# Fox attention and bilinear FFN: the late batches' scores in three TensorE visits instead of four

## The chip, the cores and the metric

The kernel runs on one core of one Trainium2 chip. The metric is the device time of one execution in microseconds (us); lower is better. The time before is the median of three runs, 402.83 us (400.74 to 403.5).

## The reference

Forgetting attention over 8 batches of 8 heads, 576 positions and 64 dimensions, followed by a bilinear feed-forward network (FFN) over the 4608 tokens:

```
scores = scale * np.matmul(q, k.transpose(0, 1, 3, 2))
cum = np.cumsum(np.log(np.clip(f, 0.0001, 1.0)), axis=-1)
scores = np.where(causal, -1000000000.0, scores + cum[:, :, :, None] - cum[:, :, None, :])
attn = exp(scores - max) / (sum + 1e-09)
x = (attn @ v)  as [4608, 512]
out = ((x @ w_a) * (x @ w_b)) @ w_out          # 512 -> 1536 -> 512
```

## The kernel before

**Tiles.** A *unit* `u` is four heads of one batch (`b, hh = divmod(u, 2)`), so there are two units for each batch; a *pair* `t` is two heads, two pairs to a unit. The 576 query positions of a head are cut into four blocks of 128 rows (blocks 0 to 3) and a tail of 64 rows (block 4). Block i needs the keys 0 to 128(i+1), the tail needs all 576. Each head's 64 dimensions lie as two halves of 32 partitions, and the four heads of a unit sit in the four 32-row groups of the array, so that the score products of the four heads run abreast.

**Visits.** TensorE computes a unit's scores in visits (`qk_group(u, g)`, matmuls at L399). `groups = [(1, 0), (2,), (3,), (4,)]` says which blocks a visit holds, so a unit takes four visits, in the order 0, 1, 3, 2 from batch 2 on. A visit writes two PSUM tiles of two banks each (`sc`, a ring of two, so one visit holds all four `sc` banks until its scores are read). The other four banks are the ring `ff`: FFN products, transposes, value products. From batch 3 on the value product of the pair's tail (`pv4`, L634) is written into 64 spare columns of the first visit's tile.

**Softmax.** Batches 0 to 2 (`DIRECT`) add the decay and the mask with further matmuls (`pick`, `low`), and VectorE takes a row maximum (L486). From batch 3 on VectorE reads the scores out of PSUM, adds the decay from the SBUF tile `spread` and takes the maximum in one custom operation (`do_decay`, L510; two for each block and pair, one for each head), into a tile `S` in SBUF; that operation is what releases the PSUM banks. ScalarE takes the exponentials (L542, L548), VectorE the reciprocals of the sums, GpSimd normalises (L565) and masks the decay rows (L460 to L471). The probabilities are transposed by DMA, and TensorE multiplies them with the values (`pv`, L609, L611), VectorE or ScalarE evicts.

**FFN.** For each block of tokens (256, 384 or 512) and each of 12 slices of 128 hidden columns TensorE makes `psa` and `psb` (four matmuls each, L872), ScalarE or VectorE copies `psa` to fp16 (L138, L142), VectorE multiplies with `psb` (L888), and 36 output rows of 12 matmuls follow (`pso`, L897). A `psa` or `psb` needs a free `ff` bank; a bank comes free with the copy or the multiplication.

**Order.** All of the work is cut into numbered operations. `ORDER` is a table of these numbers that sets, by hand, the order in which they are issued on all engines; `CHOICE` gives the engine of each operation that could go to several. Forty `fill` operations (four matmuls on an identity each, L178) are placed in it too; they compute nothing that is used. Each engine works through its own list in order.

Of the kernel before, what the change touches and what calls it, by code (L numbers as in the profile page):

```python
# [37 lines left out]
def kernel(  # L38
# [61 lines left out]
    RING = {"S": 2, "bc": 4, "n32": 3, "n16": 2, "PA": 3, "PB": 2, "PTA": 2, "PTB": 2, "st": 8, "ht": 15, "a16": 3, "osb": 2, "ff": 4}  # L100
# [88 lines left out]
    def f_tiles():  # L189
        x = [s_pool.tile([128, 1024], FP32, tag="S", name=n) for n in ("cum_f", "cum_l")]  # L190
        cw["f"], cw["l"] = x[0][HP[0], 0:S], x[1][HP[0], 0:S]
        cw["1"] = x[0][:, S:].bitcast(FP16)[:, 0:S]
# [112 lines left out]
    def batch_inputs(b):  # L305
# [4 lines left out]
        for which, part, gm in items:  # L310
            gate = qk_ops[(2 * (b - 1) + gm // 4, gm % 4)][-1:] if b >= EARLY else []
# [61 lines left out]
    groups = [(1, 0), (2,), (3,), (4,)]  # L373

# [12 lines left out]
    def qk_group(u, g):  # L387
        b, hh = divmod(u, 2)
        qT, kT = T[("T", "q", b)], T[("T", "k", b)]
        rows = crow[b // 2] if b < DIRECT else None  # L390
        if single(u, g):
            c = [[ps.tile([128, 512], FP32, tag="ff", bufs=RING["ff"], name=f"sc{g}") for _ in range(2)] for _ in range(2)]
        else:
            c = [ps.tile([128, 2, 512], FP32, tag="sc", bufs=2, name=f"sc{g}") for _ in range(2)]
        heads = [(c[w] if g == 3 else [c[w][0], c[w][1]] if single(u, g) else [c[w][:, 0, :], c[w][:, 1, :]],
# [5 lines left out]
        if g == 3:  # L401
            for x, lo, hi in ((0, 0, SF), (1, SF, S)):
# [3 lines left out]
            for x, lo, hi in ((0, 0, SF), (1, SF, S)):  # L406
                if b < DIRECT:
                    for y, h, r, n in heads:
                        mm(y[HP[h], x, 0:hi - lo], pick[r, n:n + 1].to_broadcast([32, 64]), rows[r, lo:hi], stop=True)
            if b < DIRECT:  # L410
                for a in range(2):
                    for y, h, r, _ in heads:
                        mm(y[HP[h], 1, 32 * a:32 * a + 32], low[r, a, 0:64], neg[r, :], stop=True)
            for w in range(2):
                T[("s", NP * b + 2 * hh + w, 4)] = c[w].rearrange("p a k -> p (a k)")[:, 0:S]
            return
        t0 = 2 * u
        col, n_ = 0, 0
        for i in groups[g]:
# [16 lines left out]
            if b < DIRECT and i == groups[g][-1]:  # L436
                m = len(groups[g])
                lo = 0 if turned(t0, groups[g][0]) else col - 128 * m
                hi = 128 if m == 1 and lo == 0 else col
                for a in range(4):  # L440
                    for y, h, r, _ in heads:
                        x = y[h][:, lo:hi].rearrange("p (m k) -> p m k", k=128)
                        x = x[:, 0:3:2] if hi - lo == 384 else x
# [3 lines left out]
        if g == 0 and not single(u, g):  # L447
            for w in range(2):
                T[("spare", t0 + w)] = c[w][:, 0, 448:512]
# [39 lines left out]
    def do_decay(t, g, i, h):  # L489
        st, c = stats(t), spread[t % RING["bc"]]  # L490
        if ("S", t, g) not in T:
            T[("S", t, g)] = s_pool.tile([128, 1024], FP32, tag="S", name="S")
            col = 0
            for x in groups[g]:
# [6 lines left out]
        else:  # L501
            n = 128 * (i + 1)
            o, x, y = T[("z", t, i)][:, h * n:h * n + n], T[("s", t, i)][:, h, :], c[:, h, SM:SM + n]
# [15 lines left out]
    def p_tile(t, part):  # L519
# [4 lines left out]
        if ("P", "A", t) not in T and t in IN_S:  # L524
            x = s_pool.tile([128, 1024], FP32, tag="S", name="S").bitcast(FP16)
# [137 lines left out]
    def softmax(t, g, qk, sc, rows, st_users, pu, norms):  # L663
# [4 lines left out]
        for i in groups[g]:  # L668
            part = part_of(t, i)
            mxs = []  # L670
            for h in range(1 if direct else 2):
                if direct:
                    mx = op("D", f"max{i}" + ("s" if sc[0] is not sc[1] else ""), lambda _, i=i: do_max(t, i), [qk])
# [17 lines left out]
                for x in sc if direct else sc[h:h + 1]:  # L691
# [3 lines left out]
            for h in range(1 if i == 4 else 2):  # L695
                ex = op("A", f"exp{i}", lambda _, i=i, h=h: do_exp(t, i, h), mxs if i == 4 or direct else mxs[h:h + 1])
                if direct:
                    ex.deps.append(o_e)
                    sc[h].append(ex)
# [26 lines left out]
    def attention(u):  # L726
# [5 lines left out]
        turn = (0, 1, 3, 2)  # L732
        for g in turn:
# [3 lines left out]
            qk = op("E", f"qk{g}" + ("d" if b < DIRECT else ""), lambda _, g=g: qk_group(u, g), deps)  # L737
# [6 lines left out]
            sc_of[g] = [take(qk, "sc") for _ in range(2)]  # L744
            for w in "qk":
                T_users[(w, b)].append(qk)
            if g == 0 and (u - 1) // 2 >= EARLY:
                old = [t - 2 for t in ts]
                for x, t in enumerate(old):
                    pv4 = op("E", "pv4", lambda _, t=t: do_pv4(t, T.pop(("spare", t + 2))), [qk, *late[t][0]])  # L750
                    sc_of[0][x].append(pv4)
                    behind.append((pv4, x))
                    pv = op("E", "pv", lambda _, t=t: do_pv(t, (0, 1, 2, 3)), [qk, *late[t][0]])
                    late[t][1](pv, pv4, sc_of[0][x])
        for w, t in enumerate(ts):
            for g in turn:
                softmax(t, g, qk_ops[(u, g)][0], [sc_of[g][w]] * 2, bc[t], st_users, pu, norms)
        for pv4, x in behind:
            pv4.deps.extend(o for o in sc_of[0][x] if o.kind[:3] in ("dec", "max", "exp"))
# [374 lines left out]
```

## Time and profile before

| | before |
|---|---|
| median of three runs | 402.83 us (400.74 to 403.5) |
| the profiled execution | 402.96 us, span 401.2 us |
| busy TensorE / VectorE / ScalarE / GpSimd | 386.0 / 315.3 / 250.0 / 255.1 us |
| attention ends on TensorE at | about 345 us, then FFN alone |

The span is the time from the first to the last instruction; the profiled execution's own time is 1.8 us longer. Start times in the timeline count from the span's start, and a matmul's listed duration includes its pipeline, so that what a group costs is read from start to start.

### The profile page before, as it was taken

The page shows a single profiled execution, that of the slowest core. Times are in us where ns is not written, and L with a number is a line of the kernel's source. Part 1 is how long each engine was busy: PE and PEld are TensorE (multiplying, and loading weights), DVE is VectorE, ACT ScalarE, POOL GpSimd, SP SyncE. Part 2 cuts the span into 40 slices and gives each one's busy share as a digit, 9 for nine tenths or more (in the row PEclk, how much of TensorE's full clock was granted, in tenths as well). Part 3 has the DMA queues.
Part 4 walks back from the last instruction along what each step waited for, and adds up shares of the span by engine and source line. Part 5 has one row for each costly group of instructions (what it writes and reads, how often), then busy time and mean ns, then how long its engine had stood idle before and what let it go on. Part 6 is the DMA issues. An engine that isn't in the chain of part 4 may idle for free.

```text
span 401.2 us, 11066 instructions
## 1 busy us (share of the span) xinstructions
PE 386.0 (96%) x4040; PEld 213.8 (53%) x4040; DVE 315.3 (79%) x908; ACT 250.0 (62%) x755; POOL 255.1 (64%) x425
## 2 busy tenths in 40 slices
PE   6788999989999999999999999999999999999996
PEld 6666776856755544444445444544454444444554
DVE  8789998978959889997989879789978792462560
ACT  4887876566657667868785778677868783201011
POOL 4888777988478777889597859697777472000000
PEclk9659999999999999999999999999999999999999
DMA  7999789999999898999999999989998629100102
GB/s 279 194 246 265 129 218 283 219 192 231 223 218 209 225 191 242 228 292 219 288 216 299 225 255 276 252 206 256 206 218 181 132 53 205 38 2 36 70 1 79
DMA packets 148311, 78.22 MB, mean 195 GB/s; under 512 B 130592, under 2 KB 133408, under 8 KB 148256
## 3 DMA queue, kind: packets, MB, share of 16 engines
q1 hardware_dynamic: 144416, 72.66, 77.2%
q0 software_dynamic: 3696, 4.72, 7.3%
q8 instruction: 31, 0.51, 0.5%
q14 instruction: 24, 0.20, 0.1%
q10 hardware_dynamic: 144, 0.13, 0.1%
HBM read 49.69 MB, written 9.58 MB: 148 GB/s over the span
## 4 chain that ended last, share of the span: by engine, by line
PE 80%; DVE 7%; DMA 7%; POOL 2%; issue 1%; SPq 1%; ACT 1%; DVEq 0%; POOLq 0%; ACTq 0%
PE pso L897 22%; PE psb L872 21%; PE psa L872 20%; PE sc L399 8%; DVE st L486 2%; PE pv L609 2%; DMA v<-in_v_dram 2%; PE idle L178 2%; DMA PTB<-PB 2%; DMA xT<-spread 1%; PE pv L621 1%; PE pv L611 1%; PE psP L589 1%; DMA k<-in_k_dram 1%; PE sc L634 1%
## 5 line engine op out<-in xcount | busy, mean ns | idle before, releaser
L872 PE MATMUL psb<-xT,wb 128*128 128x512 f16 (+2 forms) x528 | 115.2, 341 | 1.5 <-ACT osb L138 1.1
L872 PE MATMUL psa<-xT,wa 128*128 128x512 f16 (+2 forms) x528 | 115.2, 341 | 0.2
L897 PE MATMUL pso<-wout,ht 128*128 128x512 f16 (+1 forms) x444 | 98.0, 374 | 0.0
L565 POOL TENSOR_SCALAR PA<-PA,st 128x128 f16<-128x128 f16 (+2 forms) x162 | 75.8, 484 | 30.7 <-DVE st L557 20.5
L510 DVE CUSTOM_DVE_ANT_0 S<-sc,spread 128x128 f32<-128x128 f32 (+3 forms) x160 | 86.5, 568 | 7.5 <-PE sc L399 3.3
L888 DVE TENSOR_TENSOR ht<-psb,a 128x512 f16<-128x512 f32 (+2 forms) x132 | 76.6, 587 | 14.8 <-PE psb L872 9.9
L138 ACT CAST a<-psa 128x512 f16<-128x512 f32 (+2 forms) x85 | 44.1, 525 | 51.8 <-PE psa L872 50.0
L872 PEld LDWEIGHTS <-wb 128*128 128x128 f16 x528 | 49.8, 98 | 43.5 <-issue 4.3
L872 PEld LDWEIGHTS <-wa 128*128 128x128 f16 x528 | 49.7, 98 | 42.8 <-issue 3.0
L548 ACT ACTIVATE PA<-S,st 128x256 f16<-128x256 f32 (+2 forms) x120 | 60.1, 503 | 14.4 <-DVE st L510 13.0
L897 PEld LDWEIGHTS <-ht 128*128 128x128 f16 x444 | 41.8, 98 | 46.7 <-issue 0.6
L565 POOL TENSOR_SCALAR PB<-PB,st 128x512 f16<-128x512 f16 (+1 forms) x84 | 58.8, 716 | 11.7 <-DVE st L557 8.1
L486 DVE TENSOR_REDUCE st<-sc 128x2 f32<-128x512 f32 (+8 forms) x68 | 47.1, 726 | 8.5 <-PE sc L399 5.9
L399 PE MATMUL sc<-kT,qT 32*128 32x128 f16 (+5 forms) x960 | 42.4, 274 | 4.9 <-DVE qT L302 2.7
L399 PEld LDWEIGHTS <-qT 32*128 32x128 f16 (+1 forms) x960 | 18.6, 96 | 28.3 <-issue 13.9
L548 ACT ACTIVATE PB<-S,st 128x512 f16<-128x512 f32 x40 | 28.5, 714 | 6.3 <-DVE st L510 6.1
L557 DVE RECIPROCAL st<-st 128x2 f32<-128x2 f32 x128 | 18.2, 157 | 14.0 <-ACT PB L548 6.8
L142 DVE CAST a<-psa 128x256 f16<-128x256 f32 (+2 forms) x47 | 25.1, 534 | 4.6 <-PE psa L872 3.9
L142 POOL CAST k<-k 128x1152 f16<-128x1152 f32 (+1 forms) x15 | 20.9, 1393 | 10.8 <-DMA k<-in_k_dram 7.4
L565 POOL TENSOR_SCALAR spread<-spread,st 128x128 f16<-128x128 f16 (+4 forms) x36 | 19.8, 561 | 6.6 <-DVE st L557 5.0
L138 ACT CAST xT<-pv 128x512 f16<-128x512 f32 (+2 forms) x36 | 16.0, 465 | 12.6 <-PE pv L611 6.3
L460 POOL TENSOR_SCALAR_AFFINE_SELECT spread<-spread 128x768 f32<-128x768 f32 x20 | 17.4, 870 | 9.3 <-DMA spread<-cum_d 5.1
(99 smaller groups left out, 493.2 us busy)
## 6 DMA issues: line engine op xcount, KB each, us to landing
spread<-cum_d SPq DMA_DIRECT2D x20, 576.0 KB, 5.8
out_dram<-osb SPq DMA_DIRECT2D x35, 256.0 KB, 3.2
k<-in_k_dram SPq DMA_DIRECT2D x15, 576.0 KB, 6.2
q<-in_q_dram SPq DMA_DIRECT2D x15, 576.0 KB, 6.0
v<-in_v_dram SPq DMA_DIRECT2D x32, 256.0 KB, 6.9
wout<-in_moe_w_out_dram POOLq DMA_DIRECT2D x3, 512.0 KB, 7.2
v<-in_v_dram SPq DMA_DIRECT2D x8, 128.0 KB, 4.5
wb<-in_moe_w_b_dram POOLq DMA_DIRECT2D x1, 1024.0 KB, 15.8
```

Source lines behind the costliest of these rows:

```text
L138: nc.scalar.copy(out=out_, in_=in_)
L142: ENG[e].tensor_copy(out=out_, in_=in_)
L399: nc.tensor.matmul(out=dst, lhsT=lhsT, rhs=rhs, start=start, stop=stop, skip_group_check=True)
L460: nc.gpsimd.affine_select(out=c[:, :, 0:SM].rearrange("p h (j k) -> p h j k", k=128), in_=c[:, :, SM:2 * SM].rearrange("p h (j k) -> p h j ...
L486: nc.vector.tensor_reduce(out=m if i == 4 else st[:, 2 * i:2 * i + 2][:, h:h + 1] if isinstance(x, list) else m, in_=y, axis=AXX, op=MAX, ...
L510: nc.vector.tensor_tensor_reduce(out=o, in0=x, in1=y, scale=-1.0, scalar=3e38, op0=ADD, op1=MIN, accum_out=m)
L548: nc.scalar.activation(out=p_blocks(t, i)[:, :, h, :], in_=x.rearrange("p (j k) -> p j k", k=128), func=EXP, scale=sign, bias=st[:, c:c + ...
L557: nc.vector.reciprocal(out=st[:, 20 + 2 * i:22 + 2 * i], in_=st[:, 10 + 2 * i:12 + 2 * i])
L565: ENG[e].tensor_scalar(out=p, in0=p, scalar1=st[:, c:c + 1], scalar2=1.0, op0=MUL, op1=MUL)
L872: nc.tensor.matmul(out=o, lhsT=w16[:, db, 128 * fb:128 * fb + 128], rhs=tokens(db, t0, n), start=(db == 0), stop=(db == 3))
L888: nc.vector.tensor_tensor(out=ht[:, 0:n], in0=T.pop(("psb", t0, fb))[:, 0:n], in1=T.pop(("a16", t0, fb))[:, 0:n], op=MUL)
L897: nc.tensor.matmul(out=o, lhsT=T[("ht", t0, fb)][:, 128 * tb:128 * tb + 128], rhs=wout16[:, fb, c], start=(fb == 0), stop=(fb == 11))
```

## The change

From batch 2 on (`EARLY = 2`) a unit takes three visits, `late_groups = [(4, 1), (2, 0), (3,)]`, in this order. The first holds the tail and block 1. The tail fills one bank and 64 columns of the next of each `sc` tile; block 1 of the first head of a pair goes into 256 columns beside that, and block 1 of the second head into one bank of the ring `ff` (`d`, for each pair one, so two `ff` banks more for each such visit). The spare columns for `pv4` move from block 0's bank to the columns 320 to 384 of that second bank. The tile `S` grows from 1024 to 1088 columns, since 576 + 512 columns go in, and the ring `ht` of FFN products shrinks from 15 to 14 tiles. In batch 2 the maximum over block 1 becomes two operations for a pair, one for each head. `ORDER` and `CHOICE` are new throughout, batches 0 and 1 included; `CHOICE` has 159 operations on ScalarE, 112 on VectorE and 7 on GpSimd, before 174, 96 and 8. The number of matmuls (4040) and of fills (160 matmuls) is unchanged.

```diff
+    late_groups = [(4, 1), (2, 0), (3,)]
+    def blocks_of(t, g):
+        return (late_groups if t // NP >= EARLY else groups)[g]
...
+        late = b >= EARLY
+        last = g == (0 if late else 3)
...
+            if late:
+                d = [ps.tile([128, 512], FP32, tag="ff", bufs=RING["ff"], name="sc1") for _ in range(2)]
+                pairs = [(d[w][:, 0:256] if h else c[w][:, 1, 64:320], h, RG[2 * w + h], 8 * (b % 2) + 4 * hh + 2 * w + h)
+                         for w in range(2) for h in range(2)]
+                for n, (j0, j1) in enumerate(key_runs(t0, 1)):
+                    for dh in range(2):
+                        for y, h, r, _ in pairs:
+                            mm(y[:, 128 * n:128 * n + 128 * (j1 - j0)], qT[r, hh, dh, 128:256], kT[r, hh, dh, 128 * j0:128 * j1],
+                               start=h == 1 and n == 0 and dh == 0, stop=dh == 1)
...
+                    T[("s", t0 + w, 1)] = [c[w][:, 1, 64:320], d[w][:, 0:256]]
+                    T[("spare", t0 + w)] = c[w][:, 1, 320:384]
...
-        turn = (0, 1, 3, 2)
+        turn = range(3)
...
-            sc_of[g] = [take(qk, "sc") for _ in range(2)]
+            sc_of[g] = [[x, x] for x in (take(qk, "sc") for _ in range(2))]
+            if g == 0:
+                sc_of[g] = [[x[0], take(qk, "ff")] for x in sc_of[g]]
...
-    RING = {"S": 2, "bc": 4, "n32": 3, "n16": 2, "PA": 3, "PB": 2, "PTA": 2, "PTB": 2, "st": 8, "ht": 15, "a16": 3, "osb": 2, "ff": 4}
+    RING = {"S": 2, "bc": 4, "n32": 3, "n16": 2, "PA": 3, "PB": 2, "PTA": 2, "PTB": 2, "st": 8, "ht": 14, "a16": 3, "osb": 2, "ff": 4}
...
     ORDER = """
-        0 14 10 20 34 42 43 1 64 41 2 30 44 45 54 46 47 55 21 56 57 48 67 68 31 69 27 71 11 72 58 70 16 49
+        0 7 33 42 43 1 64 26 28 2 20 34 44 22 67 54 14 45-47 55 56 9 68 48 49 65 38 11 21 39 35 57 69 15 58
```

On TensorE, at the end of a tail visit of batch 4 in the kernel before (`sc3` is the tail's tile, `pso` an FFN output), this stands in a row:

```order
L399 MATMUL sc3_3873<-kT_3349,qT_3385 64x64
L399 LDWEIGHTS qT_3385
L399 MATMUL sc3_3874<-kT_3349,qT_3385 64x64
L399 LDWEIGHTS qT_3385
L399 MATMUL sc3_3874<-kT_3349,qT_3385 64x64
L897 LDWEIGHTS ht_3730
L897 MATMUL pso_3862<-wout16_72,ht_3730 128x512
```

At the end of the tail's part of a first visit now (`sc0` is the tile of two banks, `sc1` the bank from `ff`):

```order
L405 LDWEIGHTS qT_3402
L405 MATMUL sc0_3646<-kT_3388,qT_3402 64x512
L405 LDWEIGHTS qT_3402
L405 MATMUL sc0_3645<-kT_3388,qT_3402 128x128
L405 LDWEIGHTS qT_3402
L405 MATMUL sc1_3663<-kT_3388,qT_3402 128x128
```

The tail (64 output rows, so half of the array's columns) was followed by the FFN, which uses the whole array; it is now followed by the 16 matmuls of block 1 in the same visit, which use all 128 columns and 32-row groups.

On VectorE, behind the first visit of a unit of batch 4 before (`sc0_3647` and `sc0_3648` are the two pairs' tiles of blocks 1 and 0, `ht<-psb` the FFN's multiplication; the 1-column rows read out the maximum):

```order
L510 ISA S_3674,st_3673<-sc0_3647,spread0_78 128x256
L510 ISA st_3673 128x1
L510 ISA S_3674,st_3673<-sc0_3647,spread0_78 128x256
L510 ISA st_3673 128x1
L888 TENSOR_TENSOR ht_3679<-psb_3631,a16_3641 128x512
L510 ISA S_3683,st_3682<-sc0_3648,spread1_79 128x256
```

Behind the first visit of the same unit now (`sc1_3663` and `sc1_3664` are the two banks from `ff`):

```order
L536 ISA S_3682,st_3681<-sc0_3645,spread0_78 64x576
L536 ISA st_3681 64x1
L536 ISA S_3682,st_3681<-sc1_3663,spread0_78 128x256
L536 ISA st_3681 128x1
L536 ISA S_3686,st_3685<-sc0_3646,spread1_79 64x576
L536 ISA st_3685 64x1
L536 ISA S_3686,st_3685<-sc1_3664,spread1_79 128x256
L536 ISA st_3685 128x1
L536 ISA S_3682,st_3681<-sc0_3645,spread0_78 128x256
L536 ISA st_3681 128x1
L142 CAST a16_3711<-psa_3701 128x512
L917 TENSOR_TENSOR ht_3715<-psb_3694,a16_3713 128x512
```

Two decays of the tail, three of block 1 and a cast now stand ahead of the next multiplication, where two decays of block 1 stood before; the decays of `sc1` are what gives the two `ff` banks back.

On TensorE at the start of the program (`rows` are the decay rows of batches 0 to 2, `sc0` the first scores), this stood between the two before:

```order
L225 LDWEIGHTS xT2_68
L225 MATMUL rows_249<-wout16_72,xT2_68 128x320
L399 LDWEIGHTS qT_239
L399 MATMUL sc0_252<-kT_214,qT_239 128x256
L399 LDWEIGHTS qT_239
```

And now:

```order
L225 LDWEIGHTS xT2_68
L225 MATMUL rows_254<-wout16_72,xT2_68 128x256
L178 LDWEIGHTS ident_60
L178 MATMUL idle_265<-ident_60 128x128
L178 LDWEIGHTS ident_60
```

The scores followed the decay rows at once; now 20 fill matmuls on `ident` stand between them, and 16 instead of 32 between the first and the second scores.

More of the change, by code (lines that the diff above doesn't have):

```diff
@@ L667, in softmax @@
         su = None
-        for i in groups[g]:
+        for i in blocks_of(t, g):
             part = part_of(t, i)
+            at = [sc[0], sc[0]] if i == 4 else sc
             mxs = []
@@ L690, in softmax @@
                         su.append(mx)
[L691 removed]
+                for x in at if direct else at[h:h + 1]:
                     x.append(mx)
```

144 lines of the change are left out of this document (79 added, 65 removed), and 134 rows, old and new, of the table ORDER.

## The prediction

> **What bounds the kernel now.** I read the page first: busy shares, the slices, and the chain that ended last.
>
> ```profile
> PE 386.0 (96%) x4040; PEld 213.8 (53%) x4040; DVE 315.3 (79%) x908; ACT 250.0 (62%) x755; POOL 255.1 (64%) x425
> ...
> PE   6788999989999999999999999999999999999996
> ...
> PEclk9659999999999999999999999999999999999999
> ...
> PE 80%; DVE 7%; DMA 7%; POOL 2%; issue 1%; SPq 1%; ACT 1%; DVEq 0%; POOLq 0%; ACTq 0%
> ```
>
> TensorE (PE) is full from the twelfth slice on, and 80% of the chain is its. Only the first 40 us have idle tenths and a clock below full. The stretches tell how much room the others have:
>
> ```profile
> 0.00:20.00 20.00, 14.72 (x214) 12.71 (x215) 15.73 (x39) 12.92 (x38) 13.30 (x28) 0.83 0.92 236
> 20.00:40.00 20.00, 17.76 (x272) 12.73 (x275) 18.29 (x43) 15.93 (x50) 16.25 (x28) 0.74 1.13 256
> 40.00:60.00 20.00, 19.17 (x333) 14.60 (x328) 19.66 (x47) 16.64 (x55) 15.36 (x22) 1.00 0.82 172
> ...
> 200.00:220.00 20.00, 19.84 (x186) 9.36 (x185) 17.60 (x59) 14.10 (x44) 17.12 (x30) 1.00 1.05 258
> 260.00:280.00 20.00, 20.00 (x176) 9.12 (x175) 18.25 (x62) 15.67 (x47) 16.79 (x33) 1.00 0.99 228
> ```
>
> After the span and the matmuls come the busy times of PE, its weight loads, VectorE (DVE), ScalarE (ACT) and POOL, then the clock. In the late stretches PE has no gap, DVE about 2 us in 20. A busy PE can hide gaps, since the listed durations overlap, so I checked the starts in the timeline:
>
> ```profile
> 243.42 1.03 PE L872 MATMUL psb<-xT,wb 128*128 128x512 f16 x4
> 244.38 0.61 PE L399 MATMUL sc<-kT,qT 32*128 32x512 f16 x8
> 244.92 1.04 PE L872 MATMUL psa<-xT,wa 128*128 128x512 f16 x4
> ...
> 346.75 1.03 PE L872 MATMUL psa<-xT,wa 128*128 128x512 f16 x4
> 347.61 1.03 PE L872 MATMUL psb<-xT,wb 128*128 128x512 f16 x4
> ```
>
> In pure FFN a group of four matmuls of 512 columns takes 0.86 us, 0.216 each. Such a group ahead of a visit takes 0.96 (243.42 to 244.38): 0.10 more. The visit's eight score matmuls, four abreast, ought to take 2 x 0.216 = 0.43 and take 0.54: 0.11 more. So a change of the array's shape costs about 0.11 us on the engine that bounds the kernel, and a visit between two FFN groups costs 0.21 besides its columns. Real waits are few after 116 us; the two longest are
>
> ```profile
> 120.57 0.81 PE L872 MATMUL psb<-xT,wb 128*128 128x384 f16 x4 [1.05 <-ACT osb L138]
> 130.65 0.35 PE L634 MATMUL sc<-PTB,nv 128*64 128x64 f16 x10 [0.50 <-DMA PTB<-PB]
> ```
>
> So the late 285 us are TensorE's columns, its shape changes and some 3 us of waits; what other engines save there is worth nothing, and what they lose is worth nothing until PE waits for it.
>
> **The change part by part.** *Visits.* Columns and matmuls stay the same. I counted the stretches of one array shape (128x128, 32x128, 32x64, 128x64) in both orders: from batch 3's first visit to the end there are 107 before and 84 now. Ten visits go, which is 20 changes less; ten changes between tail and block 1 come, which the tile positions make necessary; the other 13 go because the value products now stand side by side or against a visit. 23 x 0.11 = -2.5 us. In batch 2 the visits with their mask matmuls alternate between the two widths, 28 stretches before, 30 now: +0.2. In batches 0 and 1 there are 35 before and 46 now, mostly by fills set between other work; that is the stretch in which PE has gaps to hide them (5.3 us in the first 20), so I take 0, with 11 x 0.11 = 1.2 as the upper end. If cover lacks, this is paid.
>
> The Trainium skill, in "TensorEngine Tiling (Array Packing)", Key Properties, says that changing the tiling mode, not merely the tile, drains the engine. The trace agrees with the 0.10 and 0.11 above; by that rule the change between tail and block 1 inside the merged visit has to be paid too, as counted.
>
> *The two extra `ff` banks.* Behind a merged visit PE has two `ff` banks until VectorE's decays have read block 1 of the second heads. The durations:
>
> ```profile
> L888 DVE TENSOR_TENSOR ht<-psb,a 128x512 f16<-128x512 f32 x60 | 40.7, 683 | 3.8 <-ACT a L138 1.7 <-PE psb L872 1.2
> L510 DVE CUSTOM_DVE_ANT_0 S<-sc,spread 64x576 f32<-64x576 f32 x40 | 30.1, 755 | 4.1 <-issue 2.0 <-PE sc L399 0.9 <-POOL spread L466 0.6
> ...
> L510 DVE CUSTOM_DVE_ANT_1 S<-sc,spread 128x256 f32<-128x256 f32 x40 | 16.2, 419 | 3.2 <-PE sc L399 1.4 <-POOL spread L460 0.8 <-POOL PB L565 0.5
> L510 DVE DVE_READ_ACCUMULATOR2_ANT st<- 128x1 f32 x160 | 13.3, 83 | 0.0
> ...
> L142 DVE CAST a<-psa 128x512 f16<-128x512 f32 x9 | 6.1, 680 | 0.0
> ...
> L142 DVE CAST xT<-pv 128x512 f16<-128x512 f32 x3 | 2.0, 678 | 0.0
> L142 DVE CAST xT<-sc 128x64 f16<-128x64 f32 x6 | 1.3, 223 | 1.5 <-PE sc L634 1.3
> ```
>
> In the order shown above for batch 4, two tail decays and two of block 1 stand ahead of the second bank's release: 2 x (0.755 + 0.08) + 2 x (0.419 + 0.08) = 2.7 us, with some 0.2 until the first starts 2.9. PE meanwhile fills three FFN groups: two in the free banks, one in the first `d`, free after 1.5; 3 x 0.86 = 2.6. The fourth waits 0.3. Three or more FFN groups stand behind the visit in five of the ten late units; in the other five `pso` comes first or early, where one bank lasts 12 x 0.216 = 2.6 us, and nothing waits. 5 x 0.3 = +1.5 us. The lower end is 0 (the older bank may serve), the upper a whole group for every unit, 10 x 0.86 = 8.6, for a VectorE that is behind when the visit ends: queued behind the decays are the multiplications that free the other two banks.
>
> The Trainium skill speaks against this part: "Perfetto Trace Analysis", Optimizing Tensor Performance, wants independent matmul groups to rotate through PSUM banks so that evacuation overlaps the next group. The trace agrees insofar as four `ff` banks show no gap between groups at 347 us; no run here shows two.
>
> *VectorE and ScalarE.* Counted in both orders, VectorE gets eight more 64-column evictions, five more value evictions of 512 columns and two more casts of `psa`: 8 x 0.223 + 5 x 0.678 + 2 x 0.680 = 6.5 us; its other moves (copies of transposes, inputs, outputs, the split maximum of batch 2) cancel to within 1 us. Spread over the 340 us of attention this is 0.4 in 20, where 1.75 to 2.4 are free in the late rows above. I take 0; if each of the 15 evictions came while PE waits for it, half of it, +3. ScalarE is relieved by as much, and nothing waits for that.
>
> *Masks.* The first visit now needs all of the masked decay rows on POOL; before, the tail's were due two visits later.
>
> ```profile
> L460 POOL TENSOR_SCALAR_AFFINE_SELECT spread<-spread 128x768 f32<-128x768 f32 x20 | 17.4, 870 | 9.3 <-DMA spread<-cum_d 5.1 <-issue 4.1
> ```
>
> Their loads run on a ring of four, so two units ahead, which covers one tail mask; POOL is free for 3 us in 20. I take 0; without that cover a VectorE decay waits 0.87, and that is inside the upper end above.
>
> *The start.* The fills now stand where PE sat idle:
>
> ```profile
> 7.30 1.04 PE L225 MATMUL rows<-wout,xT 32*128 32x256 f16 x6
> 11.03 0.61 PE L399 MATMUL sc<-kT,qT 32*128 32x256 f16 x8 [2.69 <-DVE qT L302]
> ...
> 8.00:10.00 2.00, 0.35 (x3) 1.00 1.01 383
> 10.00:12.00 2.00, 0.97 (x28) 0.51 1.14 318
> 18.00:20.00 2.00, 1.00 (x32) 1.00 1.24 207
> 20.00:22.00 2.00, 1.31 (x10) 0.57 1.12 288
> 28.00:30.00 2.00, 1.95 (x27) 0.50 1.26 261
> 30.00:32.00 2.00, 2.00 (x28) 0.87 1.11 212
> ```
>
> Ahead of the DMA share and the GB/s stands the clock: 1.00 from 8 us, 0.51 from 10, full again by 18, 0.57 from 20, and 0.87 from 30. Each drop follows a stretch in which PE did little. The 20 fills need 20 x 0.054 = 1.1 to 2 us and fit into the 2.69, so they delay no score. If they keep the clock, the first scores end 0.3 us earlier. But the exponentials and maxima set the pace here (VectorE 18.29 of 20), and the value of a faster clock is at most half of what PE lost: 17 us at half clock, some 14 of them busy, so 7 lost and 3.5 on the path. I take -0.7, with 0 and -3.5 as ends.
>
> The Trainium skill ("TensorE: Matmul & The Clock Gate", HAM oscillation) asks for no PE gap above some 3.4 us. The measured gap of 2.69 us is shorter and the clock fell all the same, so the trace decides; by that rule the fills would gain nothing, and my term would be 0.
>
> *Sum.* -2.5 + 0.2 + 1.5 - 0.7 = -1.5 us. Against the profiled execution, 402.96 us (span 401.2 and 1.8 around it), this is 401.5; its distance to the median of 402.83 is 0.1, so I predict 401.4. The end does not move otherwise: FFN and store close the program in both orders.
>
> **The rivals.**
>
> *Forecast (0.43): about even, 401.4.* The shape changes gain what the borrowed banks partly take back.
>
> *The start and the changes both pay (0.25).* Nothing waits behind the merged visits, and the clock stays up: -2.5 + 0.2 - 3.5 = -5.8, 397.2. For it: the gap at 8 us is filled in the order. Against it: VectorE's 18.29 and 19.66 of 20 between 20 and 60 us, and the gap at 18 to 20, which other engines cause.
>
> *Slower: the borrowed banks starve the FFN (0.22).* VectorE is still busy with the unit before when the first visit ends, and PE waits one FFN group at each of ten units: +8.6 - 2.5 + 0.2 = +6.3, 409.3. It decides where the release of the second `d` comes later than 2.6 us behind the visit, the time of three groups; I reckon 2.9, so a VectorE that is 0.6 us late, one multiplication, triples the wait. For it: 88 to 91% busy VectorE with 6.5 us more work, in whose list the five decays stand ahead of the multiplication. Against it: five units have `pso` there.
>
> *The visit is not what costs (0.10).* If the shape changes overlap with weight loads elsewhere and come back as waits for the same data, the time stays at 402.9. Against it stand the 0.10 and 0.11, which recur at each visit.
>
> **How the numbers follow.** A measurement here can tell about 1% from no change, so 398.8 and 406.9 are the bounds. Faster by over 1% is the second case, 0.25; slower is the third, 0.22; the first and the last, 0.53, lie within. The ends of the range lie at the second and third cases' own values, 397 and 409, beyond which about half of the one (0.12) and a third of the other (0.08) remain. The likeliest case's own range is 399 to 405, by its bounds of 0 and 3 us for banks, start and VectorE.
>
> **What would show it.** The visits of block 4 and 1 come as one stretch with a 32x64 and a 32x128 part, some 0.1 us lost between them; total waits of PE after 116 us stay near 3 to 5 us. Rows of `psa` or `psb` behind the merged visit with idle time put down to `S` (VectorE's decay) of over 0.5 us each show the third case. PEclk of 9 in the second and third slices shows the second case. The forecast is wrong if late waits sum to over 8 us, or if the first 60 us differ by more than 3.

## The result, and the profile after

| | before | changed |
|---|---|---|
| median of 17 runs each | 402.86 us (400.74 to 405.69) | 404.61 us (403.38 to 407.08) |
| ratio, 95% interval | | 1.0047 (1.0026 to 1.0068) |
| the profiled execution | 402.96 us, span 401.2 us | 405.92 us, span 404.1 us |
| busy TensorE / VectorE / ScalarE / GpSimd | 386.0 / 315.3 / 250.0 / 255.1 us | 383.5 / 318.8 / 244.0 / 251.7 us |

The change costs 0.5%, where the prediction had 0.4% less. It is inside the range, and within 1% of before, but it went the other way. The profiled execution of the changed kernel is 1.3 us above its own median; what follows explains its span, 2.9 us longer, of which the medians show 1.75.

The page of the changed kernel, with the rows that were read of before:

```profile
PE 383.5 (95%) x4040; PEld 211.9 (52%) x4040; DVE 318.8 (79%) x928; ACT 244.0 (60%) x740; POOL 251.7 (62%) x424
...
PE   7578999979889999999999999999999999999996
...
PEclk9979999978999999999999999999999999999999
...
PE 81%; DVE 9%; ACT 6%; DMA 2%; issue 1%; SPq 0%; ACTq 0%; DVEq 0%
```

Lower than before are the ninth, eleventh and twelfth slice (81 to 91 and 101 to 121 us; a slice is 10.1 us): TensorE has gaps again where before had an eight and two nines, and in the ninth and tenth its clock falls, which it did not before. This is batch 2. Its first merged visit starts at 81.0 us, batch 3's at 124.9; before, batch 2's first visit started at 78.1, batch 3's at 122.0.

To see how much each stretch lost, I took from the trace the start of every matmul and worked out TensorE's *lost time*: the time so far, less what its matmuls so far need at the prediction's 0.216 us for 512 columns. Fewer columns need less in proportion, but for about 0.0026 us that each matmul takes besides (in the FFN at the end, 512 columns take 0.2158 us from start to start and 384 columns 0.1625). Matmuls of 32 rows count as four abreast, the others that use 64 columns of the array as two; fills count as lost.

| stretch | before lost | changed lost | difference | the prediction's terms |
|---|---|---|---|---|
| 0 to 80 us (batches 0 and 1) | 35.7 | 37.0 | +1.3 | -0.7 |
| 80 to 120 us (batch 2) | 6.6 | 12.8 | +6.2 | +0.2 |
| 120 us to the end (batches 3 to 7, FFN) | 15.2 | 10.7 | -4.5 | -2.5 + 1.5 |

The sum, +3.0, is the difference of the spans. So in these two profiles the late part gained more than forecast, and batch 2 lost it all. How far one execution can be trusted is seen in the traces of the experiments below: ten kernels have before's order and visits from the start through batch 2, and they lose 6.6 to 8.6 us from 80 to 120 us; the two others with the changed order all through (d_first, pso_behind) lose 13.2 and 12.3. Before's 6.6 is at the low end, but batch 2 costs more in every trace of the changed order. The waits of TensorE in batch 2, engine and line waited for, sum, times, longest; first before, from 78 to 122 us:

```profile
PE pv L621 <- DMA xT<-spread: 1.2, 1, 1.2
PE psb L872 <- ACT osb L138: 1.1, 1, 1.1
PE sc L399 <- ACT PA L548: 0.4, 1, 0.4
```

and in the changed kernel from 80 to 125 us:

```profile
PE psb L901 <- ACT a L138: 1.9, 1, 1.9
PE psb L901 <- DVE ht L917: 1.1, 1, 1.1
PE psb L901 <- ACT PA L574: 0.6, 1, 0.6
PE sc L660 <- ACT PB L568: 0.6, 1, 0.6
PE sc L405 <- ACT PB L568: 0.4, 1, 0.4
PE psa L901 <- DVE ht L917: 0.3, 1, 0.3
```

The waits rise from 2.7 to 4.9 us, and four of the six are `psa` or `psb` without a bank. The longest stands behind the first merged visit. TensorE, VectorE and ScalarE there, in the timeline (start, length, engine, what, idle before and its releaser):

```profile
82.55 0.44 PE L405 MATMUL sc<-neg,xT 32*64 32x32 f16 x24
82.93 0.61 PE L901 MATMUL psb<-xT,wb 128*128 128x256 f16 x4
83.37 0.60 PE L901 MATMUL psa<-xT,wa 128*128 128x256 f16 x4
85.91 0.60 PE L901 MATMUL psb<-xT,wb 128*128 128x256 f16 x4 [1.93 <-ACT a L138]
...
83.05 2.75 DVE L510 TENSOR_REDUCE st<-sc 128x1 f32<-128x576 f32 x6 [0.43 <-PE sc L405]
85.71 0.42 DVE L917 TENSOR_TENSOR ht<-psb,a 128x256 f16<-128x256 f32 x1
...
84.31 0.74 ACT L568 ACTIVATE PB<-sc,st 128x576 f16<-128x576 f32 x1 [3.58 <-DVE st L510]
...
85.04 0.46 ACT L574 ACTIVATE PA<-sc,st 128x256 f16<-128x256 f32 x1
...
85.49 0.37 ACT L138 CAST a<-psa 128x256 f16<-128x256 f32 x1
85.74 0.49 ACT L574 ACTIVATE PA<-sc,st 128x256 f16<-128x256 f32 x1
...
86.65 0.49 ACT L574 ACTIVATE PA<-sc,st 128x256 f16<-128x256 f32 x1
```

TensorE has two `ff` banks left, fills them in 0.87 us and stops. VectorE reads six row maxima (2.75 us); the first exponential runs 1.3 us behind the first of them (84.31), and in batch 2 the exponentials read the scores in PSUM themselves (`PA<-sc`), so the borrowed banks are free only when theirs end, at 86.2 and 87.1 us. The copy that could have given back one of the other two banks stands behind two exponentials in ScalarE's queue. The stretches of 2 us that follow (after the busy times stands the clock):

```profile
84.00:86.00 2.00, 0.09 (x1) 0.09 (x1) 2.00 (x6) 1.69 (x6) 0.00 (x0) 1.00 1.24 192
86.00:88.00 2.00, 1.65 (x26) 1.06 (x26) 1.35 (x7) 2.00 (x9) 1.71 (x3) 0.70 0.69 202
88.00:90.00 2.00, 2.00 (x60) 1.86 (x59) 0.32 (x1) 0.22 (x1) 0.95 (x2) 0.50 1.21 268
...
92.00:94.00 2.00, 2.00 (x7) 0.76 (x6) 1.12 (x4) 1.41 (x7) 1.20 (x3) 0.60 0.86 151
```

After the gap the clock is halved from 86.8 to 93.6 us, with TensorE listed as busy nearly throughout; that costs an estimated 3 us (half of 6.8). In this execution waits (+2.2) and clock are about 5 of the 6.2 us; of the rest, changes of shape inside the merged visits can be a part.

In the late part the same borrowing does no harm. Batch 4's first merged visit, with the decays that stand behind it:

```profile
167.55 1.02 PE L405 MATMUL sc<-kT,qT 32*64 32x64 f16 x32
...
168.50 1.04 PE L901 MATMUL psa<-xT,wa 128*128 128x512 f16 x4
...
168.69 0.75 DVE L536 CUSTOM_DVE_ANT_0 S<-sc,spread 64x576 f32<-64x576 f32 x1 [0.28 <-PE sc L405]
...
169.38 0.41 DVE L536 CUSTOM_DVE_ANT_1 S<-sc,spread 128x256 f32<-128x256 f32 x1
...
169.38 1.03 PE L901 MATMUL psb<-xT,wb 128*128 128x512 f16 x4
...
169.72 0.74 DVE L536 CUSTOM_DVE_ANT_0 S<-sc,spread 64x576 f32<-64x576 f32 x1
...
170.40 0.41 DVE L536 CUSTOM_DVE_ANT_1 S<-sc,spread 128x256 f32<-128x256 f32 x1
...
170.74 0.41 DVE L536 CUSTOM_DVE_ANT_1 S<-sc,spread 128x256 f32<-128x256 f32 x1
...
171.10 1.03 PE L901 MATMUL psb<-xT,wb 128*128 128x512 f16 x4
```

The decays that release the two banks, the first two of 128x256, end at 169.8 and 170.8, the second 2.3 us behind the visit's end (168.50), and the fourth FFN group starts at 171.10, without a wait. From 125 us to the end this is all that TensorE waits:

```profile
PE psa L901 <- ACT a L138: 0.4, 1, 0.4
```

### The profile page after: what moved, and what is told of

It reads as the page before. It is cut to its first block, busy times and chain, and to the rows that moved or that the text cites. A ratio compares the mean times of both kernels' runs of the same rounds, so it can differ in the third digit from the quotient of the medians.

```text
span 404.1 us, 11065 instructions
## 1 busy us (share of the span) xinstructions
PE 383.5 (95%) x4040; PEld 211.9 (52%) x4040; DVE 318.8 (79%) x928; ACT 244.0 (60%) x740; POOL 251.7 (62%) x424
## 4 chain that ended last, share of the span: by engine, by line
PE 81%; DVE 9%; ACT 6%; DMA 2%; issue 1%; SPq 0%; ACTq 0%; DVEq 0%
PE pso L926 22%; PE psb L901 21%; PE psa L901 21%; PE sc L405 9%; DVE st L510 5%; ACT PA L574 3%; PE pv L635 2%; DMA q<-in_q_dram 2%; PE pv L637 1%; PE sc L660 1%; PE idle L178 1%; PE pv L647 1%; ACT PB L568 1%; DVE ht L917 1%; DVE PTB L142 1%
## 5 line engine op out<-in xcount | busy, mean ns | idle before, releaser
L591 POOL TENSOR_SCALAR PA<-PA,st 128x256 f16<-128x256 f16 (+2 forms) x162 | 75.2, 478 | 31.5 <-DVE st L583 28.7
L536 DVE CUSTOM_DVE_ANT_0 S<-sc,spread 64x576 f32<-64x576 f32 (+3 forms) x160 | 85.5, 567 | 10.6 <-PE sc L405 5.2
L138 ACT CAST a<-psa 128x512 f16<-128x512 f32 (+2 forms) x83 | 42.8, 518 | 57.0 <-PE psa L901 54.5
L574 ACT ACTIVATE PA<-S,st 128x384 f16<-128x384 f32 (+2 forms) x120 | 59.8, 500 | 18.0 <-DVE st L536 14.4
L510 DVE TENSOR_REDUCE st<-sc 128x1 f32<-128x256 f32 (+8 forms) x72 | 46.9, 693 | 10.7 <-PE sc L405 9.1
L405 PE MATMUL sc<-kT,qT 32*128 32x128 f16 (+5 forms) x960 | 40.5, 274 | 4.8 <-DVE qT L302 2.1
L138 ACT COPY osb<-pso 128x512 f32<-128x512 f32 (+1 forms) x25 | 14.1, 566 | 29.0 <-PE pso L926 27.5
L142 DVE CAST a<-psa 128x256 f16<-128x256 f32 (+2 forms) x49 | 26.8, 548 | 4.6 <-PE psa L901 3.5
L405 PEld LDWEIGHTS <-qT 32*128 32x128 f16 (+1 forms) x960 | 16.7, 97 | 24.0 <-issue 14.8
L591 POOL TENSOR_SCALAR spread<-spread,st 128x256 f16<-128x256 f16 (+4 forms) x36 | 19.5, 552 | 8.5 <-DVE st L583 8.0
```

The lines of the kernel that those rows point to most:

```text
L138: nc.scalar.copy(out=out_, in_=in_)
L142: ENG[e].tensor_copy(out=out_, in_=in_)
L405: nc.tensor.matmul(out=dst, lhsT=lhsT, rhs=rhs, start=start, stop=stop, skip_group_check=True)
L510: nc.vector.tensor_reduce(out=m if i == 4 else st[:, 2 * i:2 * i + 2][:, h:h + 1] if isinstance(x, list) else m, in_=y, axis=AXX, op=MAX, ...
L536: nc.vector.tensor_tensor_reduce(out=o, in0=x, in1=y, scale=-1.0, scalar=3e38, op0=ADD, op1=MIN, accum_out=m)
L574: nc.scalar.activation(out=p_blocks(t, i)[:, :, h, :], in_=x.rearrange("p (j k) -> p j k", k=128), func=EXP, scale=sign, bias=st[:, c:c + ...
```

## The experiments

Kernels that mix the two orders are the changed kernel with a tuple `MERGED` of the batches that use three visits, and with `ORDER` and `CHOICE` put together from both tables, operation by operation. "Before" is each time the kernel before, run beside them. Each ratio has its 95% interval; it is worked out from the single runs, not from the two medians, and can differ from their quotient by up to 0.3%.

**Which part does what?** Three kernels take one part each of the changed kernel, all else as before (`MERGED` is as here in late_only, holds 2 alone in batch2_only and is empty in start_only):

```diff
+    MERGED = (3, 4, 5, 6, 7)
...
-        return (late_groups if t // NP >= EARLY else groups)[g]
+        return (late_groups if t // NP in MERGED else groups)[g]
...
-        late = b >= EARLY
+        late = b in MERGED
```

> Batches 0 to 2 with the visits, the order and the engines of before; from batch 3's first visit on the three visits, the order and the engines of the changed kernel. Theory (the loss sits before batch 3, the late part gains what the two profiles show from 120 us on, 4.5 us): 402.9 - 4.5 = 398.4 us, ratio to before 0.989. Rival 1 (the late gain is only what was left undone earlier, FFN work that fills the late stretch): no gain, 402 to 403. Rival 2 (the prediction's own terms, -2.5 for shapes and +1.5 for banks): 401.9.

> Only batch 2 (from the first visit of its first unit to the first visit of batch 3) in the changed form; all else as before. Theory (batch 2's merged visits hold the two banks through six maxima and the exponentials, TensorE waits 3.3 us more there and loses another 3 to half the clock): 402.9 + 6 = 409 us. Rival (the merged visit costs its shape changes only, the waits come from what the new start leaves behind): 403 to 404.

> Only the start (batches 0 and 1, up to the first visit of batch 2) in the changed order; all else as before. Theory (the fills keep the clock up in the first 30 us but the exponentials set the pace; the profiles differ by 1.3 us at 80 us): 402.9 + 1.3 = 404.2 us. Rival (10 us less at half clock pay): 399.4 to 401.

Measured: late_only 408.96 us against 404.15 (1.0143, 1.0103 to 1.0182), batch2_only 412.36 (1.0229, 1.0188 to 1.0270), start_only 405.41 (1.0052, 1.0026 to 1.0077). The second goes as the theory has it; lost time from 80 to 120 us in batch2_only is 15.9 us instead of 6.6, more than the 6 expected; that its order begins on what another start has left can be a reason. The third has the time that its theory names, but not by the theory's way: its trace has lost 36.3 us by 80 us, 0.6 more than before, and 11.0 from there to 120 us, most of it in one wait of 4.1 us for a transposition at the joint of the two orders. So it does not tell what the start costs. The first misses by 10 us. Its trace shows why, at the joint of the two orders:

```profile
129.34 1.44 PE L906 MATMUL psb<-xT,wb 128*128 128x384 f16 x4 [5.19 <-DVE st L541]
...
127.14 1.21 DVE L303 STREAM_TRANSPOSE kT<-k 128x576 f32<-128x576 f32 x1 [3.68 <-POOL k L143]
128.19 0.73 DVE L541 CUSTOM_DVE_ANT_0 S<-sc,spread 64x576 f32<-64x576 f32 x1
```

I had put a cast and a transpose ahead of the first merged visit's decays; TensorE stood for 5.19 us, and the clock fell for 6.8. That is the price of the joint, and it hides what the kernel was made to show. What follows the joint is in line, though: from 140 us to the end TensorE loses 10.0 us in late_only, and 9.6 in the changed kernel, d_first and pso_behind; with four visits it is 12.3 (before), 12.9 (start_only), 13.0 (ht14), 13.8 (form_b2) and 14.2 (batch2_only).

**Is it the order within batch 2?** d_first puts the maxima and exponentials of block 1, which release the borrowed banks, ahead of the tail's; pso_behind does so too, and moves FFN output work, which needs one bank for long, behind the merged visits:

```diff
-        1680 464 459 1682 1679 1681 1684 467 471 468 472 338 1686 437 405 473 495 499 1685 409 1683 500 501
+        1680 464 459 1682 1679 1681 1684 471 499 473 501 1686 472 500 1685 1683 467 495 468 338 437 405 409
```

The numbers are operations: 464 is the merged visit, 471 and 499 are block 1's maxima, 467 and 495 the tail's, 473 and 501 the exponentials that release the two banks. The second unit is changed alike. In pso_behind 1692, 1693 and 1697 to 1699 are the output work that moves:

```diff
+        1680 464 459 1682 1679 1681 1692 1693 1684 471 1683 499 473 472 501 500 1686 467 495 468 1685 338 437
...
-        463 617 1710-1712 1709 601 1713 527 1714 1716 1715 538 542-544 618 1718 566 570-572 567 539
+        463 617 1710-1712 1709 601 1713 527 1714 1697-1699 1716 1715 542 570 544 543 1718 1717 572 571 538 566
```

> The changed kernel, with the row maxima and exponentials of block 1, which release the two borrowed banks, ahead of the tail's in batch 2's two units (VectorE's and ScalarE's order there; TensorE's is the same). Theory (the banks are held too long): the wait of 1.93 us at 86 us falls below 0.7, the clock stays full after it, 404.6 - 1.3 - 3 = 400.3 us. Rival (VectorE's 2.7 us of maxima set the pace whatever their order, and the wait moves to the next use of a bank): 404 to 405, with the same sum of waits from 80 to 120 us (6.0).

> The changed kernel with FFN output work, which needs one bank for up to 12 matmuls, moved behind the merged visits of batch 2: two of three parts of one output row behind the first, a whole row behind the second; and with the maxima and exponentials of block 1 ahead of the tail's, an FFN multiplication between them. Theory (TensorE waits in batch 2 because it has only two banks while VectorE and ScalarE read the visit): the waits from 80 to 120 us fall from 6.0 to below 3 us, the clock stays full, 404.6 - 3 = 401.5 us or less. Rival (batch 2's maxima and exponentials set the pace, work that is moved is missing later): 404 to 406, waits about 6 us, at other places.

Measured: 405.88 against 404.15 (1.0056, 1.0026 to 1.0085) and 405.57 against 403.73 (1.0049, 1.0026 to 1.0071), both as slow as the change itself, within the noise. The 1.93 us at 86 us went in both; the waits in batch 2 came back elsewhere. (The 6.0 in the expectations was too high; the list above sums to 4.9.) In d_first:

```profile
PE sc L660 <- ACT PB L568: 2.5, 1, 2.5
PE sc L405 <- ACT PB L568: 2.3, 2, 1.8
PE psb L901 <- DVE ht L917: 1.1, 1, 1.1
PE psb L901 <- ACT PA L574: 0.5, 1, 0.5
```

6.4 us in all, now for the tail's exponentials, which hold the `sc` banks of the next visit. In pso_behind it is 7.2. Both rivals come near (d_first is 0.9 us above its rival's 405, beside a before that is 1.3 us above its first median). It fits them that whichever bank is let go first, the next one in the line is waited for, so that batch 2's maxima and exponentials set the pace for the work that the order puts between its visits; two tries argue for this and do not show it, and in pso_behind 3.2 of the 7.2 us are waits for a copy by VectorE and for a transposition. From batch 2's first visit to batch 3's it takes 43.9 us in before and 43.9 in the changed kernel, but at its end the changed kernel stands five FFN groups and an output group further back (4.1 us of TensorE).

**Is it the form?** Before's order and engines everywhere, with the merged visits put in place of the old ones: tail and block 1 where 1 and 0 stood, block 2 with 0 where 2 stood, the tail's own visit dropped. form_b2 does so in batch 2 (the line here), form_late in batches 3 to 7, form_all in all six:

```diff
+    MERGED = (2,)
```

> The same for batch 2 alone: before's order and engines, merged visits only in batch 2's two units. Theory (the form costs: the two borrowed banks stay taken through six maxima and four exponentials, and each visit has five array changes inside): waits of TensorE from 78 to 122 us rise from 2.7 to 6 us or more, ratio 1.010 to 1.016. Rival (the new order is what fits badly, the form costs six array changes): 0.8 us, ratio 1.002.

> The order and the engines of before throughout; from batch 3 on the merged visits in it: tail and block 1 where block 1 and 0 stood, block 2 with 0 where block 2 stood, block 3 in its place, the tail's own visit gone; the softmax steps of block 0 and the tail change places. Theory (20 array changes fewer, banks back in time): TensorE's excess from 125 us to the end 2 to 4 us less than before, ratio 0.990 to 0.996. Rival 1 (the late gain is the new order's, with FFN output work placed behind the visits): waits for a bank behind the merged visits, ratio 1.00 to 1.02. Rival 2: no difference.

> Both together: before's order and engines, merged visits from batch 2 on, which is the change without its new order. Theory (parts add up): batch 2 loses 4 to 6 us, the late part gains 2 to 4, ratio 1.002 to 1.008, as the change itself. Rival (the new order is needed to hide the banks): 1.015 or more.

Measured: form_b2 409.81 us against 403.57 (1.0145, 1.0113 to 1.0177). The waits of TensorE from 77 to 124 us begin with

```profile
PE psb L906 <- ACT PA L579: 2.9, 1, 2.9
PE psa L906 <- ACT PA L579: 1.3, 1, 1.3
PE pv L652 <- ACT PA L579: 1.1, 1, 1.1
```

5.3 of 6.3 us are waits for block 1's exponentials, that is, for the borrowed banks. Part of the 2.9 belongs to this order and not to the form: there the tail's exponential stands ahead of them in ScalarE's queue, and it starts only at 108.09, after 3.80 us for the transposition that empties its buffer. form_late took 446.59 us (1.1079, 1.1049 to 1.1109) and form_all 453.78 (1.1257, 1.1221 to 1.1292), with waits at nearly every unit, the largest in form_late 9.8 us in six pieces for transposed probabilities; in both, the tail's exponentials of five pairs are written before the pair two before has been transposed, so part of the attention is not the reference's. Rival 1 was right as to the order: the late form needs an order of its own. On whether that form is cheaper these two say nothing.

**Does the late form gain?** late_only2 mends the joint, from4 and from5 put it at batch 4 and at batch 5, where both orders have done nearly the same FFN work. from5b is from5 with the load of one pair's decay rows ahead of their mask; in from5 that mask is laid on the rows that stood there before, so that pair is not the reference's. ht14 shortens the ring `ht` alone. The edits of from5b and of ht14:

```diff
+    MERGED = (5, 6, 7)
...
-    RING = {"S": 2, "bc": 4, "n32": 3, "n16": 2, "PA": 3, "PB": 2, "PTA": 2, "PTB": 2, "st": 8, "ht": 15, "a16": 3, "osb": 2, "ff": 4}
+    RING = {"S": 2, "bc": 4, "n32": 3, "n16": 2, "PA": 3, "PB": 2, "PTA": 2, "PTB": 2, "st": 8, "ht": 14, "a16": 3, "osb": 2, "ff": 4}
```

> As late_only, with the joint at batch 3's first visit mended: the mask of the first pair's tail right behind the mask of its rows, the casts and transposes of kT's second half behind the visit, and the FFN work that the earlier part is ahead (six groups) taken out evenly of the block of 384 tokens that follows. Theory (late visits are cheaper, the loss lies before batch 3): the 5.2 us wait at the joint goes, TensorE's excess over its ideal time grows by 10 to 11 us from 120 us to the end (12 to 15 before), 402.9 - 3 = 400 us, ratio below 0.995. Rival (the late gain was FFN work left over from earlier): ratio 0.998 to 1.005.

> Before's order, engines and visits up to the first visit of batch 4; from there the changed kernel's visits, order and engines, with three FFN groups that the earlier part is ahead taken out evenly of the 512 tokens in work. Theory (late merged visits are cheaper, 8 of the 10 units): TensorE's excess from 170 us to the end 8.5 to 9.5 us (11.0 before), ratio 0.994, faster than both kernels. Rival (the gain from 120 us on was batch 3 alone, or FFN work left over): ratio 1.00.

> The same with the joint at batch 5, where both orders have done the same FFN work (6 of the 10 units). Theory: 1.6 us less than before, ratio 0.996; no wait over 0.7 us behind the joint. Rival: ratio 1.00 or above.

> As from5, with the load of one pair's decay rows ahead of their mask, which stood the wrong way round at the joint. Theory (late merged visits are cheaper, 6 of 10 units): TensorE's excess from 220 us to the end about 5.9 us against 7.2 of before, no wait over 0.7 us behind the joint, 1.3 to 1.6 us less than before, ratio 0.996 to 0.998, the fastest of the kernels. Rival: ratio 1.00 or above.

> The kernel before with 14 instead of 15 tiles for the FFN products, nothing else. Theory (the ring is long enough): within 0.2%. Rival (the fifteenth tile is needed where FFN work runs ahead): 1.003 or more, with waits of VectorE's multiplication for a tile.

Measured: late_only2 413.25 against 403.73 (1.0235, 1.0205 to 1.0264), a miss: its thinned FFN work leaves TensorE waiting, between 140 and 160 us, for the next transposed probabilities:

```profile
PE sc L665 <- DMA PTB<-PB: 6.9, 1, 6.9
```

from4 408.51 against 403.67 (1.0123, 1.0080 to 1.0166), a miss too, again with waits behind the joint (6 us). from5 402.33 against 403.67 (0.9980, 0.9951 to 1.0010), from5b 402.77 against 403.37 (0.9996, 0.9965 to 1.0026), ht14 403.21 against 403.67 (1.0011, 0.9983 to 1.0040). The joint of from5b holds: from 195 us on TensorE waits twice, for 0.6 and 0.3 us. From 220 us to the end it loses 5.7 us, before 7.2, the changed kernel 5.5. So the trace shows the gain that was expected, 1.5 us, and it is no accident of one execution: from 220 us on, the eight traces with the late part of the changed kernel (itself, d_first, pso_behind, late_only, late_only2, from4, from5, from5b) lose 5.3 to 5.9 us, and the five with before's (before, ht14, start_only, form_b2, batch2_only) 7.2 to 8.8. That is the form together with its order; no run here separates the two. The times of the runs (before and from5b each scatter by some 5 us) neither confirm nor exclude a gain of this size, and from5b cannot be told from before. The ring of 14 costs nothing that can be measured.

**What does a visit cost besides its columns?** 20 more visits of eight score-shaped matmuls (128 columns, read by nobody) in the FFN that runs alone at the end, one behind each of 20 groups, or all at one place:

```diff
+        for dh in range(2):
+            for x in range(4):
+                nc.tensor.matmul(out=c[x // 2][:, x - x // 2 * 2, 0:128], lhsT=qT[RG[x], 0, dh, 0:128],
+                                 rhs=kT[RG[x], 0, dh, 0:128], start=dh == 0, stop=dh == 1, skip_group_check=True)
```

> The kernel before with 20 more score-shaped visits (eight matmuls of 32 rows and 128 columns each, four abreast, read by nobody) in the FFN that runs alone at the end, one behind each of 20 FFN groups. Theory (a change of shape costs 0.10 to 0.11 us, so a visit between two FFN groups 0.21 besides its columns): 20 x (0.107 + 0.21) = 6.3 us more than before. Rival (the change overlaps with weight loads when it recurs): 2.1 us more.

> The same 20 visits, all at one place. Theory: 20 x 0.107 + 0.21 = 2.4 us more than before, so 4.0 less than with the visits apart. Rival: the same 2.1 us as apart.

Measured against 403.73: apart 410.83 (1.0189, 1.0147 to 1.0231), together 412.65 (1.0222, 1.0185 to 1.0259). Two visits of the first kernel with the group between them, and then all of the second with what follows:

```profile
349.20 0.29 PE L985 MATMUL dm<-kT,qT 32*128 32x128 f16 x8
349.43 1.04 PE L872 MATMUL psa<-xT,wa 128*128 128x512 f16 x4
350.40 0.29 PE L985 MATMUL dm<-kT,qT 32*128 32x128 f16 x8
```

```profile
348.98 7.98 PE L985 MATMUL dm<-kT,qT 32*128 32x128 f16 x160
356.89 1.89 PE L872 MATMUL psa<-xT,wa 128*128 128x512 f16 x4
```

Apart, a group and a visit take 1.20 us (349.20 to 350.40) instead of 0.86: 0.34, of which 0.11 are columns, so 0.23 for the two changes of shape, as at the visits of the late part. Over all 20 places it is 0.22 each. The single starts in the trace show that the eight do run abreast, four within 0.01 us and the next four 0.06 later, so that the 0.22 are not slow matmuls. The price holds and adds up. The second kernel was to be the control and is none: it took 7.9 us for 160 matmuls instead of 2.4, since each of its visits waits for the one before (the last section says more).

## Why the prediction was wrong

**The step that failed** is, as the prediction put it: "In batch 2 the visits with their mask matmuls alternate between the two widths, 28 stretches before, 30 now: +0.2." Batch 2 was priced by its changes of shape alone. The borrowed banks were priced only for "the ten late units", by VectorE's decays; batch 2 has merged visits too, and has no decays. There VectorE reads six maxima, and the banks come free only with ScalarE's exponentials, which read PSUM directly. The kernel before shows it: its `do_exp` reads the scores' own tile where `direct` holds, and its trace has the exponentials of those batches as reading `sc`. It was not followed up. Measured: +6.2 us in the profile, and 1.0145, or 5.9 us, when the form is put into batch 2 of before's order (a part of this belongs to that order, as said above). None of the prediction's signs of being wrong looked there: they watch the first 60 us and the waits after 116 us, and batch 2 lies between.

**Visits, -2.5.** Right in price: 0.22 for each visit between FFN groups, added 20 times over. The change inside a merged visit is paid too, as counted: batch 4's takes 0.95 us (167.55 to 168.50), its columns need 0.71, and the 0.24 left are about two changes, one inside and one behind it. From 140 us on the changed kernel loses 2.7 us less than before.

**The two extra banks, +1.5 in the late part.** Too high: TensorE waits 0.4 us in all from 125 us on. The reckoning added the decays' listed durations to 2.7; start to start the same four take 2.05 (168.69 to 170.74), because each of them overlaps with its read-out and the next (decays start 0.69 apart, at 168.69 and 169.38, where the first is listed with 0.75). The release comes 2.3 us behind the visit, inside the 2.6 that three groups need. The mechanism of the slower rival, banks that starve the FFN, was right; it placed it in the ten late units, where its own point of decision, 2.6 us, is not reached, and not in batch 2, where it is passed.

**Late waits.** The prediction took 3 us of late waits as they were; the trace of before lists 1.9 after 116 us (1.1, 0.5 and 0.3). From 120 to 140 us the changed kernel loses 1.8 us less than before, whose two longest waits (1.05 and 0.50) lie there; with the 2.7 this makes the 4.5. This 1.8 can't be put down to the change: batch2_only, which has before's order from batch 3 on, loses as little there (1.2 us, the changed kernel 1.1), other traces of before's order up to 3.5.

**The start, -0.7.** Not gained. The fills did keep the clock: before it is at half for 17 us in the first 31, now for 6.8, from 18.5 to 25.3 us. Nothing was gained by it: at 40 us both have lost 28.5. It fits this that VectorE and ScalarE set the pace there, as the prediction said and then only half believed. By 80 us the new order is 1.3 us behind in the two profiles. The four traces with the new start have lost 36.1 to 37.0 us by then, twelve of the thirteen with before's 34.9 to 35.8, and one, ht14, 37.0: about 1 us, no more than what one execution of the same start can add.

**The clock** was counted only at the start. The fall at 86.8 us follows a gap of 1.93 us on TensorE (0.09 of 2 us busy from 84 to 86). The Trainium skill ("TensorE: Matmul & The Clock Gate", HAM oscillation) asks for no gap above some 3.4 us; as with the 2.69 us before the first scores, the trace has the clock fall after a shorter one. But this fall is not what sets the two kernels apart. Among the ten traces with before's order and visits through batch 2 the clock falls at 86 to 88 us in four (late_only, from4, from5b, tail_together; 3.4 us each, behind gaps of 1.8 to 2.4 us), which lose 7.9 to 8.6 us from 80 to 120 us; in the six others (gaps of 1.1 to 1.9 us) it does not, and they lose 6.6 to 7.4. In pso_behind it stays full throughout batch 2, and 12.3 us are lost there all the same. So the fall costs part of the time in the executions that have it, gaps just under 2 us go either way, and the cost of the merged visits is there without it. Among the 17 runs, those with a mean clock of 0.99 and more took 403.4 to 404.6 us, those with 0.983 took 405.1 to 405.9, which is about as much as the profiled run lies above the median.

**Not settled:** whether an order exists in which batch 2's merged visits cost nothing. Two tries within the changed order failed. It was not tried to give batch 2 its four visits back within the changed order; the kernels with the old batch 2 and the new late part from batch 3 on failed at their joints.

## What to carry to other kernels

When a buffer is borrowed from a ring, price its release in every stage that borrows it, by what reads it there: one stage's reader (a decay of 0.4 us) may be another's two engines in a row (2.75 us of maxima, then exponentials). Take the time of a queue of short instructions from start to start, not by adding durations. And a hand-made order is worth more than the form it carries: mixed orders lost 4 to 10 us at a joint that looked harmless, so an experiment that mixes two must show its joint in the trace before its time says anything.

## What the runs showed of the hardware that was not expected

- The busy time that the profile lists for TensorE can hide waits. In the series of 20 visits at one place (160 matmuls, listed as one row of 7.98 us without a gap), the single starts in the trace show that each visit's eight matmuls start within 0.12 us, and that then nothing starts for 0.23 us: each visit writes the same PSUM tiles as the one before, and its first matmul waits for a semaphore that TensorE's own matmuls of the visit before raise. The listed durations, 0.21 to 0.23 us each at the full clock, cover the gap. The weight loads show it, eight by eight (idle time before them in brackets):

```profile
349.67 0.15 PEld L985 LDWEIGHTS <-qT 32*128 32x128 f16 x8 [0.19 <-issue]
350.02 0.15 PEld L985 LDWEIGHTS <-qT 32*128 32x128 f16 x8 [0.19 <-issue]
```

Within one visit there are no such gaps: in the kernel before, 24 matmuls of 32 rows and 128 columns in a row take 0.45 us, a change of shape among it, and their starts lie 0.06 us apart for every four:

```profile
184.34 0.51 PE L399 MATMUL sc<-kT,qT 32*128 32x128 f16 x24
184.79 2.76 PE L897 MATMUL pso<-wout,ht 128*128 128x512 f16 x12
```

- The clock fell in that series, 3.4 us behind its start (348.98 to 352.40), though TensorE is listed as busy (busy time, PE first, and the clock ahead of the last two columns):

```profile
350.00:352.00 2.00, 1.90 (x48) 0.92 (x48) 0.00 (x0) 0.00 (x0) 0.00 (x0) 1.00 0.03 8
352.00:354.00 2.00, 1.92 (x46) 0.95 (x40) 0.00 (x0) 0.00 (x0) 0.00 (x0) 0.60 0.00 0
```

So the listed busy time does not tell whether the clock stays full. Whether the waits between the visits let it fall, or the few columns of the matmuls, these runs don't separate.
